# Gated linear attention with a max-out layer: state products of two batches on four array tiles, a turned head order, five permuting blocks, and a last output in two pieces

## The chip, the cores and the metric

The kernel runs on one core of a Trainium2 chip. A core has a matrix engine (TensorE, "PE" in the profile, with its weight loads as "PEld"), VectorE (DVE), ScalarE (ACT), GpSimd (POOL), SyncE (SP), which here only issues transfers, and 16 DMA engines. The metric is device microseconds (us) of one execution; lower is better. "The time before" is the median of three runs of the old kernel.

## What is computed

```python
def _attn_ref(q, k, v, f_logit):            # 4 batches, 8 heads, 768 positions, 48 per head
    f = 1.0 / (1.0 + np.exp(-f_logit))
    for t in range(S):
        state = f[:, :, t, :, None] * state + np.einsum('bhd,bhe->bhde', k[:, :, t], v[:, :, t])
        y[:, :, t] = np.einsum('bhd,bhde->bhe', q[:, :, t], state)

def _moe_ref(x, w1, w2, w_out):             # x: 3072 tokens by 384
    g = np.maximum(x @ w1, x @ w2)          # 384 by 1024
    return g @ w_out                        # 1024 by 384
```

The heads of a token stand side by side in x (8 times 48 is 384).

## The kernel before

**Windows.** The sequence is cut into 3 windows of 256 positions. A unit of work `s` is one window of one batch, `s = 4 * window + batch`, so there are twelve, and `s % 2` is the parity of the batch. Position pairs stand on 128 partitions (row p holds positions 2p and 2p+1), and a window has two halves `h` of 64 rows.

**Steps.** Every step is a letter. For each unit, `Lf Lk Lq Lv` (L111) load the four inputs, 128 rows by 8 heads by 96 numbers of float32, which is 1024 runs of 384 bytes. `E F G` (ACT, L207 to L217) make the gate's logarithm and `e` its pair sum; `C` (L222) sums it up with a triangular matrix; `X Z` (ACT) take exponentials of the sums; `i j K Q` (DVE or POOL) scale k and q into the padded bf16 tiles `kp` and `qp`, and `V` (L260) casts v into `vb`. Each head takes 64 columns there, of which 48 are used. `t u` (L264) transpose `kp` and `qp` in 16 matmuls each, and `U` copies both out of PSUM into `trs`. `A` (L280) multiplies keys with queries, `m` masks the product. `S` (L308) multiplies the carried state with the queries, `y` (L328) adds the masked product times v, `z` (L323) is a tiny DVE read of the last element that `S` wrote, which stands between `S` and `y`. `D n N` (L341 to L371) bring the state forward; `S` needs the state of the unit 4 earlier (its second half) and of its own first half. `Y` copies the finished y out of PSUM into `xT`.

**Layout of x.** Heads stand in four pairs. A pair takes 128 rows: head r of the pair sits at rows 64r to 64r+47, and 16 rows of each half are a gap. The first three pairs are the three 128-row blocks of the layer's contraction; the fourth pair's 2 times 48 rows are put into the gaps of these three, by step `M` (two DMAs inside SBUF, L401), or for the first two units by matmuls (`xf`, L391). The weights must stand in the same row order: `wp` (L495) permutes the rows of w1 minus w2 by matmuls, one for each (block of the result, block of the source) that meet, listed in `meets` (L186, 7 of them), for each of 4 quarters of the columns; `wx` (L463) does it for w2's transpose by copies.

**The layer.** max(a, b) is b plus relu(a - b), so `d` (L407, four steps a unit, 6 matmuls each) multiplies x with w1 minus w2, `r` (L415) takes the relu out of PSUM, and `o` (L425, two a unit) sums x times m2 (`wm`: w2 times w_out, L479) and the relu times w_out. `b` copies an output half of 128 by 384 out of PSUM, and `O` (L440) stores both halves of a unit.

**Array tiles.** `A`, `y` and `D` address the 128 by 128 array as four 64 by 64 tiles: rows by one index (r or h), columns by the other. In `S` the row tile and the column tile are the same index r, so of the four tiles only (0,0) and (1,1) are used:

```python
rows = slice(r * DP, r * DP + D)
nc.tensor.matmul(out=ys[s][h][r * DP:(r + 1) * DP, j, :], lhsT=st[rows, j, :],
                 rhs=t[rows, h, 1, j].rearrange("p a t -> p (a t)"), ...)
```

`S` of a unit is 16 matmuls of 128 columns, 8 for the first four units, which have no state in their first half: 160 in all.

**The order of the work.** `ORDER` (L20 to L54) is a list of 558 words: step, unit, engine (a, v, p, s) and, after the @, the PSUM bank or the input slot. Each engine works its own words off in this order, and one wait in an engine's queue holds up all that is behind it. SP issues all loads, nearly all `M` and all stores, in order. There are 25 input slots of one load each; the weights pass through them first.

Of the kernel before, what the change touches and what calls it, by code (L numbers as in the profile page):

```python
# [20 lines left out]
Lf0s@12 Lk0s@13 Lq0s@14 Lv0s@15 E0 Lf1s@16 F0 Lk1s@12 e0v G0 i0v C0@0 j0v Lq1s@17 X0 Z0 K0v Lv1s@18  # L21
Q0v t0@0 V0v u0@0 E1 Wb0s U0v@0 F1 Wa0s A0.0@0 e1p G1 Wb1s m0.0v@0 Wa1s i1p C1@2 Wo0s D0@4 Wo1s X1
j1v A0.1@0 Z1 K1p n0.0v V1a m0.1v@0 S0@6 Lf2s@16 z0v@6 Q1v y0 D1@0 t1@2 Yt0a@6 wc0p n1.0v wc1a u1@2
n1.1v U1v@2 wt0@0 N1.1p xf0@6 Y0a@6 ws0p n0.1v A1.0@2 A1.1@4 m1.0v@2 wx0a@0 wt1@1 ws1p wp0@6 m1.1v@4
wc2a S1@2 Lq2s@17 z1v@2 wq0v@6 y1 wt2@0 Yt1a@2 wp1@4 ws2v d0.0@6 wq1a@4 ws3p wx2v@0 xf1@2 d0.1@7
Y1a@2 wx1v@1 wp2@4 r0.0a@6 wc3v d1.0@2 Lk2s@0 wo0p wq2a@4 wt3@1 d1.1@3 wx3v@1 N0.1p wo1a d1.2@4 wo3p
Lf3s@1 r1.0v@2 wp3@0 wo2p d0.2@6 E2 wq3v@0 Lv2s@4 wm1@2 F2 Lk3s@5 d0.3@7 G2 e2v wn1a@2 j2v C2@3
wm0@0 X2 i2v Lf4s@6 Z2 K2v r0.1a@6 Lq3s@8 Q2v t2@2 d1.3@5 E3 wn0v@0 u2@2 F3 wm2@1 V2p Lf6s@10 U2v@2
G3 e3p r1.1a@4 D2@6 Lq4s@4 wn2v@1 A2.0@2 i3p C3@0 n2.0v o0.1@1 n2.1v X3 m2.0v@2 Lk4s@1 Z3 K3p E4
S2@6 A2.1@2 Lv3s@17 F4 o1.0@0 z2v@6 j3v G4 e4p m2.1v@2 E6 Lf5s@5 C4@4 Q3v t3@2 F6 y2 Lk6s@10 j4v  # L30
u3@2 Y2a@6 o0.0@5 e6p U3v@2 X4 M2s Z4 i4v A3.0@2 b1.0a@0 Lv4s@8 K4p b0.0v@5 C6@4 G6 Lq6s@6 o1.1@0
m3.0v@2 V3a X6 Lf8s@17 Q4v t4@2 Z6 A3.1@6 b0.1a@1 N2.1p b1.1v@0 D3@4 u4@2 E5 i6p n3.0v d2.0@0 Lk5s@4
n3.1v F5 U4v@2 d2.2@4 K6p d2.1@1 G5 Lq5s@5 m3.1v@6 d2.3@5 r2.0a@0 S3@2 V4p Lv6s@10 z3v@2 r2.1a@4 y3
j6v A4.0@0 D4@6 e5v Y3a@2 o2.0@4 n4.0v N4.0v E8 M3s Q6p n4.1v m4.0v@0 A4.1@6 F8 S4@2 Lv5s@8 C5@5
Lk8s@17 G8 m4.1v@6 o2.1@0 i5p Lf7s@6 b2.0a@4 Z5 z4v@2 e8v X5 y4 K5v C8@1 Y4a@2 d3.0@4 j5v t6@6
b2.1v@0 Q5p Z8 M4s t5@2 u6@6 d3.1@5 X8 U6v@6 V5a Lq8s@4 d3.2@0 Lk7s@1 N3.1p r3.0a@4 u5@2 Lq7s@8 D5@6
i8p U5v@2 d3.3@1 E7 N4.1p d4.0@4 Lf9s@5 n5.0v r3.1a@0 A5.0@2 N5.0v d4.1@5 n5.1v F7 m5.0v@2 N5.1p
d4.2@0 O1s V6p Lv8s@6 A5.1@6 r4.0a@4 d4.3@1 m5.1v@6 e7p Lv7s@0 S5@2 r4.1a@0 D6@4 K8p A6.0@6 z5v@2 y5
n6.0v O0s m6.0v@6 C7@0 Y5a@2 o4.0@1 Lq11s@10 N6.0p G7 n6.1v X7 j8v o3.0@2 b4.0a@1 Lf11s@17 Q8v Z7 E9
j7v M5s t8@0 A6.1@4 V8v F9 S6@6 i7p m6.1v@4 u8@0 Lq9s@6 o3.1@3 V7a e9p z6v@6 U8v@0 y6 K7v A8.0@0  # L40
D8@4 Y6a@6 o4.1@5 Q7p b3.0v@2 M6s m8.0v@0 b3.1a@3 C9@2 Lv11s@1 b4.1a@5 t7@6 n8.0v D7@0 Lk9s@8 Z9
u7@6 Lf10s@0 n7.0v d5.0@4 X9 N7.0p E11 d5.2@2 N6.1v N8.0p n7.1v Lv9s@5 d5.1@5 F11 j9v d6.0@0 j11v G9
d5.3@3 r5.0a@4 e11p U7v@6 Lk11s@17 d6.1@1 Q9p r5.1a@2 d6.2@4 r6.0v@0 O4s C11@6 Lv10s@4 d6.3@5 X11
A7.0@0 Z11 i9p O2s A7.1@2 o5.1@7 m7.0v@0 E10 K9p r6.1a@4 Lk10s@0 m7.1v@2 S7@0 F10 Lq10s@6 S8@4 z7v@0
A8.1@2 G11 e10p y7 o6.1@6 Y7a@0 i11v K11v M7s C10@0 Q11p m8.1v@2 o6.0@1 Z10 G10 z8v@4 X10 V11p y8
b6.0a@1 t11@2 b6.1v@6 Y8a@4 t9@0 u11@2 u9@0 o5.0@6 U11v@2 U9a@0 M8s j10v O6s d7.0@2 O3s Q10v b5.0a@6
A9.0@0 b5.1a@7 A9.1@4 i10p d7.1@3 m9.0v@0 V9a d7.2@6 K10p r7.0a@2 m9.1v@4 d8.0@0 d7.3@7 V10p d8.1@1
r7.1v@6 t10@4 r8.0a@0 D9@2 D11@3 u10@4 n9.0v A11.0@6 N7.1v U10a@4 A11.1@0 o7.0@2 n11.0v N11.0p N9.0v
d8.2@4 b7.0v@2 o7.1@3 m11.0v@6 m11.1v@0 d8.3@5 S9@6 r8.1a@4 b7.1v@3 S11@0 z9v@6 O7s D10@3 y9 z11v@0
# [9 lines left out]
def kernel(  # L59
# [22 lines left out]
    HD = H * D  # L82
    d_ff = moe_w1.shape[1]
# [3 lines left out]
    GAP = DP - D  # L87
# [23 lines left out]
    def load(nm, s, slot):  # L111
        w, b = divmod(s, B)
        src = sources[nm][b, :, w * W:(w + 1) * W, :].rearrange("h (p two) d -> p h (two d)", two=2)
        nc.sync.dma_start(out=slots[:, slot, :].rearrange("p (h x) -> p h x", h=H), in_=src)  # L114
        loaded[s][nm] = slots[:, slot, :].rearrange("p (h two d) -> p h two d", h=H, two=2)
# [52 lines left out]
    perm = consts.tile([C, KT, KT, C], BF16, name="perm")  # L168
    nc.gpsimd.memset(perm, 0.0)
    for j in range(KT):  # L170
        for r in range(2):
            first = D * (2 * j + r)
            for blk in range(KT):
                lo, hi = max(first, blk * C), min(first + D, (blk + 1) * C)
                if lo < hi:
                    nc.vector.tensor_copy(perm[:, blk, j, r * DP + lo - first:r * DP + hi - first],
                                          ident[:, lo - blk * C:hi - blk * C])
    for r in range(2):
        first = (2 * KT + r) * D - (KT - 1) * C
# [80 lines left out]
    def step_V(s, e):  # L260
        copy(e, pad("vb", s)[:, :, :, 0:D], by_parity(loaded[s]["v"]))
# [45 lines left out]

    def step_S(s, b):  # L308
        t = tr[s]
        ys[s] = [banks[:, b + h, :].rearrange("p (j t) -> p j t", j=NP) for h in range(2)]  # L310
        for h in range(2):
            if not has_state(s, h):
                continue
            st = state_before(s, h)
            for j in range(NP):
                for r in range(2):
                    rows = slice(r * DP, r * DP + D)
                    nc.tensor.matmul(  # L318
                        out=ys[s][h][r * DP:(r + 1) * DP, j, :], lhsT=st[rows, j, :],
                        rhs=t[rows, h, 1, j].rearrange("p a t -> p (a t)"),  # L320
                        start=(j == 0), stop=False, skip_group_check=True)
# [6 lines left out]
    def step_y(s):  # L328
        m, vb = at.pop(s), pad("vb", s)
        for j in range(NP):  # L330
            for par in range(2):
                for r in range(2):
                    for h in range(2):
                        rows = slice(h * HC, (h + 1) * HC)
                        first = j == 0 and par == 0 and not has_state(s, h)
                        nc.tensor.matmul(  # L336
                            out=ys[s][h][r * DP:(r + 1) * DP, j, :], lhsT=vb[rows, par, 2 * j + r, :],
                            rhs=m[rows, j // 2, r, j % 2, par, :], start=first,
                            stop=(j == NP - 1 and par == 1), skip_group_check=True)
# [85 lines left out]
    def step_o(g, par, b):  # L425
        cols = slice(par * C, (par + 1) * C)
        ps = banks[:, b, 0:HD]
        for kt in range(KT):
            nc.tensor.matmul(out=ps, lhsT=x_flat(g)[:, kt, cols], rhs=m2[:, kt, :],  # L429
                             start=(kt == 0), stop=False)  # L430
        for ff in range(FG):
            nc.tensor.matmul(out=ps, lhsT=gT[g][:, ff, cols], rhs=wo[:, ff, :],  # L432
                             start=False, stop=(ff == FG - 1))
# [29 lines left out]
    def store_w2T(q, e, b):  # L463
        h, x = divmod(q, 2)
        if h not in w2T:
            w2T[h] = work.tile([C, FG // 2, HD], BF16, name="ob", tag="ob", bufs=3)
        dst = w2T[h][:, 2 * x:2 * x + 2, :].rearrange("p f (k r i) -> p f k r i", k=KT, r=2)
        src, whole = w2_rows(b), 2 * KT * D
        copy(e, dst.rearrange("p f k r i -> p f (k r) i")[:, :, :, 0:D],
             src[:, :, 0:whole].rearrange("p f (g i) -> p f g i", i=D))  # L470
        for r in range(2):
            copy(e, dst[:, :, :, r, D:DP],
                 src[:, :, whole + r * D:whole + (r + 1) * D].rearrange("p f (i k) -> p f k i", k=KT))
# [21 lines left out]
    def permute(q, b):  # L495
        started = set()
        for i, (kt, blk) in enumerate(meets):
            bank, off = divmod(kt * QF, 512)
            nc.tensor.matmul(out=banks[:, b + bank, off:off + QF], lhsT=perm[:, blk, kt, :],  # L499
# [71 lines left out]
```

## Time and profile before

| what | value |
|---|---|
| time before, median of 3 runs | 146.18 us (145.88 to 146.31) |
| profiled execution | 145.86 us |
| its span, first to last instruction | 144.1 us |
| PE / DVE / ACT / POOL busy | 124.3 / 102.3 / 82.5 / 62.1 us |
| mean granted TensorE clock | 0.995 |
| DMA | 29.14 MB, 55607 packets, 50528 of them under 512 bytes |

The profile is of one execution. "Busy" is the union of an engine's instructions. A PE matmul's duration is that of the pipelined instruction, from its start to the end of its output, so that several overlap; what a matmul costs in a dense row is the distance from start to start, which the chain of waits gives. The profiled execution is 1.8 us longer than its span, and 0.32 us below the median of the runs.

### The profile page before, as it was taken

The page shows a single profiled execution, that of the slowest core. Times are in us where ns is not written, and L with a number is a line of the kernel's source. Part 1 is how long each engine was busy: PE and PEld are TensorE (multiplying, and loading weights), DVE is VectorE, ACT ScalarE, POOL GpSimd, SP SyncE. Part 2 cuts the span into 40 slices and gives each one's busy share as a digit, 9 for nine tenths or more (in the row PEclk, how much of TensorE's full clock was granted, in tenths as well). Part 3 has the DMA queues.
Part 4 walks back from the last instruction along what each step waited for, and adds up shares of the span by engine and source line. Part 5 has one row for each costly group of instructions (what it writes and reads, how often), then busy time and mean ns, then how long its engine had stood idle before and what let it go on. Part 6 is the DMA issues. An engine that isn't in the chain of part 4 may idle for free.

```text
span 144.1 us, 5338 instructions
## 1 busy us (share of the span) xinstructions
PE 124.3 (86%) x2332; PEld 91.0 (63%) x2332; DVE 102.3 (71%) x181; ACT 82.5 (57%) x120; POOL 62.1 (43%) x63
## 2 busy tenths in 40 slices
PE   0134888999999999996999999898999999999990
PEld 0024676886656676684866688566787777768650
DVE  5887888697888888955798965687985895316120
ACT  3636553887897968596585496666955211512300
POOL 7005758830783986294746159398501000000000
PEclk9999999999999999999999999999999999999998
DMA  4999999999999799699999569993420051005005
GB/s 117 268 262 267 386 384 376 310 245 268 261 266 258 179 275 241 176 251 265 265 290 272 137 165 265 273 337 83 148 89 5 21 209 25 0 14 223 0 6 212
DMA packets 55607, 29.14 MB, mean 202 GB/s; under 512 B 50528, under 2 KB 52512, under 8 KB 55584
## 3 DMA queue, kind: packets, MB, share of 16 engines
q1 hardware_dynamic: 55456, 28.76, 76.9%
q8 instruction: 18, 0.29, 0.9%
q10 hardware_dynamic: 128, 0.05, 0.1%
q14 instruction: 5, 0.04, 0.1%
HBM read 23.59 MB, written 4.72 MB: 197 GB/s over the span
## 4 chain that ended last, share of the span: by engine, by line
PE 52%; DMA 22%; ACT 9%; SPq 6%; issue 4%; DVE 2%; POOL 1%; ACTq 0%
PE banks L412 15%; PE banks L432 14%; DMA slots<-in_f_logit_dram 11%; DMA slots<-in_moe_w_dram 6%; PE banks L429 6%; DMA slots<-in_v_dram 5%; SPq L114 4%; PE banks L336 3%; PE banks L288 2%; PE banks L271 2%; PE banks L499 2%; PE banks L318 2%; PE banks L482 2%; ACT ell L213 2%; ACT one L217 1%
## 5 line engine op out<-in xcount | busy, mean ns | idle before, releaser
L412 PE MATMUL banks<-xT,wd 128*128 128x256 bf16 x288 | 35.3, 273 | 1.4 <-ACT gT L421 1.4
L432 PE MATMUL banks<-wo,gT 128*128 128x384 bf16 x192 | 35.1, 326 | 0.0
L296 DVE TENSOR_TENSOR at_m<-banks,mask 128x1024 bf16<-128x1024 f32 x24 | 28.8, 1219 | 5.4 <-PE banks L288 5.3
L412 PEld LDWEIGHTS <-wd 128*128 128x128 bf16 x288 | 27.0, 98 | 5.9 <-DMA xT<-xT 1.7
L421 ACT ACTIVATE gT<-banks 128x1024 bf16<-128x1024 f32 x19 | 19.1, 1020 | 16.5 <-PE banks L412 16.4
L432 PEld LDWEIGHTS <-gT 128*128 128x128 bf16 x192 | 18.8, 98 | 12.4
L103 DVE COPY ob<-banks 128x384 f32<-128x384 f32 (+2 forms) x20 | 8.3, 446 | 12.2 <-PE banks L432 10.8
L429 PE MATMUL banks<-m,xT 128*128 128x384 bf16 x72 | 15.7, 327 | 0.0
L103 ACT CAST xT<-banks 128x1024 bf16<-128x1024 f32 (+2 forms) x11 | 9.4, 857 | 10.9 <-PE banks L336 9.1
L103 ACT COPY ob<-banks 128x384 f32<-128x384 f32 (+2 forms) x16 | 7.1, 466 | 14.7 <-PE banks L432 11.3
L220 POOL TENSOR_TENSOR e<-ell 128x384 bf16<-128x384 f32 x8 | 8.8, 1094 | 15.1 <-ACT ell L213 14.4
L103 DVE COPY trs<-banks 128x2048 bf16<-128x2048 bf16 x10 | 12.2, 1222 | 3.7 <-PE banks L271 3.1
L209 ACT ACTIVATE gate<-slots 128x768 f32<-128x768 f32 x12 | 10.2, 849 | 7.6 <-DMA slots<-in_f_logit_dram 7.6
L254 POOL TENSOR_TENSOR kp<-slots,inv 128x768 bf16<-128x768 f32 x7 | 12.7, 1815 | 2.6 <-DVE slots L243 1.4
L371 POOL TENSOR_TENSOR st<-tmp_s,dec 128x192 bf16<-128x192 f32 x10 | 5.8, 587 | 14.4 <-DVE tmp_s L366 14.4
L288 PE MATMUL banks<-trs 48*64 48x128 bf16 x384 | 10.4, 227 | 1.5 <-DVE trs L103 1.3
L257 POOL TENSOR_TENSOR qp<-slots,dec 128x768 bf16<-128x768 f32 x5 | 9.6, 1913 | 4.1 <-DVE slots L247 4.1
L224 PE MATMUL banks<-e,u_inc 128*128 128x384 bf16 x12 | 4.3, 356 | 7.7 <-DVE e L220 6.7
L213 ACT ACTIVATE ell<-gate 128x768 f32<-128x768 f32 x12 | 10.1, 842 | 0.5
L336 PE MATMUL banks<-at_m,vb 64*64 64x128 bf16 x384 | 8.8, 225 | 1.6 <-DVE look L326 1.6
L288 PEld LDWEIGHTS <-trs 48*64 48x64 bf16 x384 | 7.1, 110 | 3.6 <-DVE trs L103 1.7
L336 PEld LDWEIGHTS <-vb 64*64 64x64 bf16 x384 | 7.1, 111 | 3.4 <-issue 3.3
(74 smaller groups left out, 189.5 us busy)
## 6 DMA issues: line engine op xcount, KB each, us to landing
slots<-in_f_logit_dram SPq DMA_DIRECT2D x12, 384.0 KB, 6.2
slots<-in_k_dram SPq DMA_DIRECT2D x12, 384.0 KB, 6.1
slots<-in_q_dram SPq DMA_DIRECT2D x12, 384.0 KB, 6.1
slots<-in_v_dram SPq DMA_DIRECT2D x12, 384.0 KB, 5.6
out_dram<-ob SPq DMA_DIRECT2D x12, 384.0 KB, 3.4
slots<-in_moe_w_dram SPq DMA_DIRECT2D x4, 768.0 KB, 9.1
slots<-in_moe_w_out_dram SPq DMA_DIRECT2D x2, 768.0 KB, 13.7
xT<-xT SPq DMA_DIRECT2D x18, 24.0 KB, 3.4
```

Source lines behind the costliest of these rows:

```text
L103: (nc.scalar.copy if e == "a" else engines[e].tensor_copy)(out, in_)
L209: nc.scalar.activation(flat(gate[s]), flat(loaded[s]["f"]), AF.Exp, bias=0.0, scale=-1.0)
L213: nc.scalar.activation(flat(ell[s]), flat(gate[s]), AF.Ln, bias=1.0, scale=1.0)
L254: engines[e].tensor_mul(pad("kp", s)[:, :, :, 0:D], by_parity(loaded[s]["k"]), both(inv[s]))
L257: engines[e].tensor_mul(pad("qp", s)[:, :, :, 0:D], by_parity(loaded[s]["q"]), both(dec[s][:, 0:HD].rearrange("p (h d) -> p h d", h=H)))
L288: nc.tensor.matmul(out=ps[h * HC:(h + 1) * HC, j % 2, par, :], lhsT=t[rows, h, 0, j, par, :], rhs=t[rows, h, 1, j].rearrange("p a t -> p ( ...
L296: nc.vector.tensor_mul(at[s][:, jj].rearrange("p r j a t -> p (r j) (a t)"), banks[:, b:b + 2, :].rearrange("p r (j x) -> p (r j) x", j=2) ...
L336: nc.tensor.matmul(out=ys[s][h][r * DP:(r + 1) * DP, j, :], lhsT=vb[rows, par, 2 * j + r, :], rhs=m[rows, j // 2, r, j % 2, par, :], start ...
L412: nc.tensor.matmul(out=ps[:, f, :], lhsT=wd[:, kt, ff * C:(ff + 1) * C], rhs=x_flat(g)[:, kt, :], start=(kt == 0), stop=(kt == KT - 1))
L421: nc.scalar.activation(dst, src, AF.Relu)
L429: nc.tensor.matmul(out=ps, lhsT=x_flat(g)[:, kt, cols], rhs=m2[:, kt, :], start=(kt == 0), stop=False)
L432: nc.tensor.matmul(out=ps, lhsT=gT[g][:, ff, cols], rhs=wo[:, ff, :], start=False, stop=(ff == FG - 1))
```

## The change

1. **Heads of odd batches are loaded turned by three.** The head that stands at place p of an odd unit is head p + 3 (mod 8). The load is two DMAs, of 5 and of 3 heads.
2. **State products of two units together, on four tiles.** Heads are paired anew: (0,1), (6,7), (4,3), (2,5). In an even unit the two heads of a pair stand at even and odd places, in an odd unit, by the turn, at odd and even ones. So the even unit uses array tiles (0,0) and (1,1), the odd one (1,0) and (0,1). The step `S` of the even unit now issues the matmuls of both units, alternating; `S` of the odd unit issues none and only takes its banks. The number of matmuls is the same.
3. **Five permuting blocks for seven.** With the new pairs only 5 (result, source) blocks meet. The fourth pair is dealt into the gaps in another way, and for it `V` gets a second copy of a quarter of its elements with the columns re-dealt (12 more copies in all), and `wx` has four copies for three.
4. **The last output half in two pieces.** `o11.1` makes 256 columns and `o11.2` 128, each with its own copy out of PSUM, and the last unit is stored in three DMAs (`P`) and not one.
5. **A new `ORDER`** of 562 words, with other engines for some steps, other slots and banks. The units go in pairs: 2 and 3, 4 and 5, and so on.

```diff
+    tiles = [(0, 1), (6, 7), (4, 3), (2, 5)]
+    TURN = 3
+    def spot(s, head):
+        pos = (head - TURN) % H if s % 2 else head
+        return pos // 2, pos % 2
...
-        nc.sync.dma_start(out=slots[:, slot, :].rearrange("p (h x) -> p h x", h=H), in_=src)
+        if s % 2:
+            nc.sync.dma_start(out=dst[:, 0:H - TURN, :], in_=src[:, TURN:H, :])
+            nc.sync.dma_start(out=dst[:, H - TURN:H, :], in_=src[:, 0:TURN, :])
+        else:
+            nc.sync.dma_start(out=dst, in_=src)
...
-    meets = [(0, 0), (0, 2), (1, 0), (1, 1), (1, 2), (2, 1), (2, 2)]
+    meets = [(0, 0), (0, 2), (1, 2), (1, 0), (2, 1)]
...
     def step_V(s, e):
+        dst, src = pad("vb", s), by_parity(loaded[s]["v"])
+        copy(e, dst[:, :, :, 0:D], src)
+        a, b = sorted(sum(p * x for p, x in zip(spot(s, head), (2, 1))) for head in tiles[KT])
+        copy(e, dst[:, :, a:b + 1:b - a, 0:D].rearrange("p two h (i k) -> p two h k i", k=KT),
+             src[:, :, a:b + 1:b - a, :].rearrange("p two h (k i) -> p two h k i", k=KT))
...
-            for j in range(NP):
-                for r in range(2):
-                    rows = slice(r * DP, r * DP + D)
+            for x in range(NP):
+                for g in (s, s + 1):
+                    for r in range(2):
+                        j, q_ = spot(g, tiles[x][r])
+                        rows = slice(q_ * DP, q_ * DP + D)
+                        nc.tensor.matmul(
+                            out=ys[g][h][r * DP:(r + 1) * DP, x, :], lhsT=state_before(g, h)[rows, j, :],
+                            rhs=tr[g][rows, h, 1, j].rearrange("p a t -> p (a t)"),
+                            start=(x == 0), stop=False, skip_group_check=True)
...
-            engines[e].dma_start(out=x[r * DP + D:(r + 1) * DP, 0:KT, :],
+            engines[e].dma_start(out=x[r * DP + D:(r + 1) * DP, 0:KT, :][:, ::1 - 2 * r, :],
...
+    def piece(g, i):
+        return (i, slice(0, HD)) if i == 0 or g < n_s - 1 else (1, (slice(0, 2 * C), slice(2 * C, HD))[i - 1])
...
+    def step_P(g, i, e):
+        par, m = piece(g, i)
+        w, b = divmod(g, B)
+        row = b * S + w * W
+        engines[e].dma_start(out=out[row:row + W, :].rearrange("(p two) m -> p two m", two=2)[:, par, m],
+                             in_=obs[g][:, par, m])
```

The new order in the places that the prediction speaks of (words of other steps left out):

```
Lf2 Lf3 Lk2 Lq2 Lq3 E2 F2 Lk3 E3 e2p Lv2 C2 d1.2 K2v Lv3 d1.3 wm1 Lf4 C3 t2 Lf5 u2 wm2 i3p U2v Lk4 K3p A2.0 A2.1 V2a
o1.0 Lv4 Q3p V3a D2 Lq4 D3 t3 u3 o0.0 Lk5 U3v Lf7 A3.0 C4 S3 S2 Lq5 A3.1 y2 o0.1 Lv5 C5 y3 t4 D4 Lq7 u4 o1.1 A4.0 Lf6
A4.1 d2.0 Lk7 d2.2 Lk6 d2.1 d2.3 O0 d3.0 Lv7 C7 d3.1 Lq6 t5 D5 u5 o2.0 Lf9 d3.2 A5.1 O1 A5.0 Lv6 d3.3 o2.1 Lf8 S5 S4
t7 C6 y5 y4 u7 o3.0 A7.0 E9 D7 t6 o3.1 F9 u6 d4.0 E8 d5.0 F8 d4.1 d5.2 r4.0v d5.1 d5.3 r5.0a ...
... o10.1 r11.1a o10.0 o11.0 b10.0v b10.1v O10s o11.1 b11.0a P11.0s o11.2 b11.1v P11.1s b11.2a P11.2s
```

In the old order the loads after the weights go `Lf2 Lq2 Lk2 Lf3 Lv2 Lk3 Lf4 Lq3 Lf6 Lq4 Lk4 Lv3`, and the list ends `o11.0 r10.1a o10.1 b11.0v o10.0 o11.1 b10.0v b10.1v O10s b11.1a O11s`.

More of the change, by code (lines that the diff above doesn't have):

```diff
@@ L26 @@
[L26 to L37, printed above, removed]
@@ L498, in permute @@
             bank, off = divmod(kt * QF, 512)
-            nc.tensor.matmul(out=banks[:, b + bank, off:off + QF], lhsT=perm[:, blk, kt, :],
+            nc.tensor.matmul(out=banks[:, b + bank, off:off + QF], lhsT=perm[:, i, :],
                              rhs=wdn[q][:, blk, :], start=bank not in started,
```

137 lines of the change are left out of this document (74 added, 63 removed).

## The prediction

> **What bounds the kernel now.** First the head of the page: busy shares, and the span in 40 slices of 3.6 us.
>
> ```profile
> span 144.1 us, 5338 instructions
> ...
> PE 124.3 (86%) x2332; PEld 91.0 (63%) x2332; DVE 102.3 (71%) x181; ACT 82.5 (57%) x120; POOL 62.1 (43%) x63
> ...
> PE   0134888999999999996999999898999999999990
> ...
> PEclk9999999999999999999999999999999999999998
> DMA  4999999999999799699999569993420051005005
> ```
>
> PE is full from slice 7 (25 us) to the last but one, at full clock. The DMA engines are full from slice 1 to about slice 25 (94 us). So two resources press: transfers decide when the inputs of a unit are there, and PE has work for nearly the whole time behind that. Next the arrivals, in the timeline (start, duration, what; in brackets the idle time and what ended it).
>
> ```profile
> 30.00 0.84 ACT L209 ACTIVATE gate<-slots 128x768 f32<-128x768 f32 x1 [0.41 <-DMA slots<-in_f_logit_dram]
> ...
> 35.67 1.20 POOL L103 CAST vb<-slots 128x768 bf16<-128x768 f32 x1 [5.50 <-DMA slots<-in_v_dram]
> ...
> 65.30 0.84 ACT L209 ACTIVATE gate<-slots 128x768 f32<-128x768 f32 x1 [0.71 <-DMA slots<-in_f_logit_dram]
> ...
> 67.09 0.81 PE L412 MATMUL banks<-xT,wd 128*128 128x256 bf16 x6 [1.43 <-ACT gT L421]
> ```
>
> Unit 2's f comes at 30.0 us, its v as the fourth load after that at 35.67: 5.67 / 4 = 1.42 us a load. The last two rows show how an arrival reaches PE: ACT stood before a gate, the relu behind it in ACT's queue was late, and PE stood 1.43 us. Last the chain of waits, whose pieces (start, length, what) give each step's cost in dense work:
>
> ```profile
> 26.05 0.33 PE banks L394 x6
> ...
> 30.18 0.76 PE banks L499 x7
> 30.94 0.66 PE banks L412 x6
> 31.59 1.30 PE banks L482 x8
> ...
> 33.55 0.16 PE banks L224
> 33.71 0.09 PE banks L227 x4
> ...
> 38.28 0.37 PE banks L350 x32
> ...
> 76.92 0.45 PE banks L318 x16
> 77.36 0.34 PE banks L271 x16
> ...
> 79.60 0.60 PE banks L336 x32
> ...
> 103.23 0.57 PE banks L288 x32
> ...
> 114.04 1.00 PE banks L318 x29
> ...
> 138.47 0.49 PE banks L429 x3
> 138.96 1.31 PE banks L432 x8
> ```
>
> So `d` costs 0.66, `wm` 1.30, `C` 0.25, `D` 0.37, `S` 0.45 (16 matmuls), `t` or `u` 0.34, `y` 0.60, the two `A` of a unit 0.57, `o` 1.80. All PE steps of the old order at these costs: 48 `d` 31.7, 24 `o` 43.2, twelve units' `C`, `t`, `u`, `A`, `y` 25.2, `D` 3.7 (the last four units have one half), `S` 4.5, `wp` 3.0, `wm` 3.9, and 36 matmuls of `wt` and `xf` at 0.055, 2.0: about 117 us. The last matmul ends at 138.96 + 1.31 = 140.3. The 23 us between are mostly the start. Of the work 17 us stand ahead of unit 2's `C` in the order, so from there (33.55) on 100 us of work take 106.7: some 6 us are lost. Work taken off PE is therefore nearly all gained, unless the inputs are late.
>
> **The change, part by part.**
>
> *State products.* Now 0.45 / 16 = 28.1 ns a matmul (34.5 in the row at 114.04). The nearest row for four tiles is `A`, also 48 rows and 128 columns: 0.57 / 32 = 17.8 ns. 160 matmuls times 10.3 ns: **-1.7 us**. Bounds: 0, if four go no faster than two (a loss is out, as neither number nor size grows), and 160 * (28.1 - 11.6) = -2.6, at `D`'s 0.37 / 32. I take `A`, which has the same shape.
>
> One thing differs from `A`: there the two row tiles write two banks, in `S` the row tiles 0 and 1 write one bank, on different partitions, before as after. The 128-column matmul on the whole array takes 0.33 / 6 = 55 ns (L394), and `S` 28.1, so the two already run side by side in one bank. The Trainium skill, TensorEngine Tiling (Array Packing), Gotcha 1, says that different row tiles cannot access the same PSUM bank at the same time; by that `S` would cost 55 ns a matmul now, and the trace does not agree. If such a limit came in with four tiles, this term would be 0 and the time the 145.8 us of the third rival.
>
> *Permuting blocks.* 0.76 / 7 = 0.109 us each, 2 fewer in 4 quarters: **-0.9 us**, bounds 0 and -0.9. It is gained ahead of `C2`, which in its turn waits for f: 30.0 + 0.84 + 0.84, and 1.0 for `e2` on POOL (L213 and L220 below), make 32.7 us at the least; with latencies I take 32.9, against 33.55. So PE is there 0.7 us sooner, and what it saves beyond that is `d` and `wm` work done early.
>
> *Inputs of units 2 and 3 together.* In the new order v of unit 2 is the sixth load after f (before: the fourth), v of unit 3 the seventh: 30.0 + 7 * 1.42 = 39.9 us, and `V3a`, on ACT, then takes its copy and the second one. The costs are in the groups of instructions (line, engine, output and input, count; busy us, mean ns of one; idle before).
>
> ```profile
> L254 POOL TENSOR_TENSOR kp<-slots,inv 128x768 bf16<-128x768 f32 x7 | 12.7, 1815 | 2.6 <-DVE slots L243 1.4 <-ACT inv L234 1.0
> L103 DVE COPY trs<-banks 128x2048 bf16<-128x2048 bf16 x10 | 12.2, 1222 | 3.7 <-PE banks L271 3.1 <-ACT gT L421 0.6
> ...
> L213 ACT ACTIVATE ell<-gate 128x768 f32<-128x768 f32 x12 | 10.1, 842 | 0.5
> L257 POOL TENSOR_TENSOR qp<-slots,dec 128x768 bf16<-128x768 f32 x5 | 9.6, 1913 | 4.1 <-DVE slots L247 4.1
> ...
> L220 POOL TENSOR_TENSOR e<-ell 128x384 bf16<-128x384 f32 x8 | 8.8, 1094 | 15.1 <-ACT ell L213 14.4 <-POOL st L371 0.6
> L243 POOL TENSOR_TENSOR slots<-slots,one 128x384 f32<-128x384 f32 x8 | 8.0, 998 | 2.5 <-ACT one L217 1.1 <-DMA slots<-in_k_dram 0.9 <-ACT ob L103 0.4
> ...
> L103 ACT COPY ob<-banks 128x384 f32<-128x384 f32 x13 | 6.2, 483 | 14.7 <-PE banks L432 11.3 <-DVE st L371 3.3
> ...
> L371 POOL TENSOR_TENSOR st<-tmp_s,dec 128x192 bf16<-128x192 f32 x10 | 5.8, 587 | 14.4 <-DVE tmp_s L366 14.4
> ...
> L103 ACT CAST vb<-slots 128x768 bf16<-128x768 f32 x5 | 4.2, 837 | 0.1
> ...
> L103 ACT CAST xT<-banks 128x256 bf16<-128x256 f32 x2 | 0.7, 372 | 2.8 <-PE banks L336 2.8
> ```
>
> The copy of 192 elements is between nothing and the 0.37 of 256 elements on ACT; I take 0.3. `D3` cannot start before 39.9 + 0.84 + 0.3 = 41.0. PE, dense from `C2` at 32.9, has two `d`, two `wm`, `C3`, `t2`, `u2`, `A2`, `o1.0` and `D2` ahead of it, 7.6 us: it is there at 40.5. `u3` waits for `i3`, `K3` and `Q3`, all on POOL behind k of unit 3: 30.0 + 5 * 1.42 = 37.1, and 1.0 + 1.8 + 1.9 make 41.8, and PE is there at about 41.7. With the latencies between I put the stop at **+1.1 us**; bounds 0 and 2.8, the two loads by which v2 is later, with no cover by `o1.0`.
>
> *V's second copies.* 12 copies, 8 on ACT at 0.3 and 4 on POOL at up to 0.59: 2.4 us each. ACT is busy 57% and POOL 43%; the waits of both hide them, except where `D` stands behind `V` as above. Uncovered they are at most 0.3 each on PE. The fourth copy of `wx` is on DVE in the time of the weights, in which the f of unit 2 is awaited: 0.
>
> *Split loads.* 24 loads become two DMAs; the bytes and the 384-byte runs stay.
>
> ```profile
> L114 SPq DMA_DIRECT2D slots<-in_q_dram x12: 368/1323/3923, 1.9 to 93.2; - x12
> ...
> 1.25 0.56 SPq L114 DMA_DIRECT2D slots<-in_k_dram  x1
> ...
> 31.29 1.31 SPq L114 DMA_DIRECT2D slots<-in_k_dram  x1
> ```
>
> The first row has the durations in ns (least, median, most). An issue costs 0.37 to 0.56 us where nothing is in its way (the least; the kernel's second load) and 1.3 in the dense stretch, where the queue takes a load only as fast as it moves one. Two free issues, 0.74 to 1.12, are still below 1.42. Cost **0**; if the cover is gone, 0.37 to 0.56 a load on everything behind it on SP, loads, `M` and stores alike (second rival).
>
> *The last output.* Both orders keep 1.8 us of matmuls for the last half: 11 of 256 columns at 0.109 and 11 of 128 at 0.055. Behind the last matmul stand the copy, the store, and what ends the program.
>
> ```profile
> out_dram<-ob SPq DMA_DIRECT2D x4, 384.0 KB, 2.5
> ...
> xT<-xT ACTq DMA_DIRECT2D x2, 24.0 KB, 1.9
> ```
> ```profile
> 142.00:142.50 0.50, 0.00 (x0) 0.00 (x0) 0.00 (x0) 0.00 (x0) 0.00 (x0) 1.00 1.03 412
> 142.50:143.00 0.50, 0.00 (x0) 0.00 (x0) 0.00 (x0) 0.00 (x0) 0.00 (x0) 0.73 0.24 92
> ```
>
> In the windows (last three columns: clock, DMA share, GB/s) data flow at full rate up to 142.5 and are through by 142.6, 1.5 us before the end; a smaller last piece shortens the part ahead of that. Copy: 0.483 for 384 columns, 0.372 for 256, so 0.26 for 128 (the same slope): -0.2. Store: 2.5 us from issue to landing for 384 KB; 1.9 for the smallest transfer of the trace. The new last piece has 64 KB, nearest the small one: 2.0, -0.5; but 128 KB leave just ahead of it, +0.1. Sum **-0.6**, bounds -0.8 and 0.
>
> *Other changes of place.* The rest of the order is new too. I find no cost in it: the pair's `S` has `o0.0`, `o2.0`, 3.9 us of `d`, `d6` and `o7.1` between the later unit's `u` and its use, more than the 1.22 us of a copy of `trs` on DVE, and a `t`, `C`, `d` or `o` between `S` and most `y`. Value 0, open by about 1.5 us either way, as the 6 us that PE now loses after 33.55 can shrink or grow.
>
> **Sum.** -1.7 - 0.9 + 1.1 + 0 - 0.6 = -2.1 us on the profiled execution of 145.86 (span 144.1, 1.8 around it): 143.8, span 142.0. That execution is 0.32 below the median of the runs, 146.18; I give the median: **144.1 us**.
>
> **The rivals.**
>
> 1. *Late inputs swallow it.* `o1.0` needs all of m2 and unit 1's relus; if these are late, nothing covers v2, the stop is 2.8 us, and what `wp` saved is waited away too (+0.4): 146.2. For: 5.50 us of POOL waiting for one v. Against: PE has `d` and `wm` there in both orders.
> 2. *The split loads hold up the stream*, slower. By `E8` 13 odd loads have gone since f2; if each costs SP its second issue of 0.56 openly, f8 comes 7.3 us late. Unhindered it is number 27 behind f2 (stores counted): 30.0 + 27 * 1.42 = 68.3. ACT's turn for `E8` comes, by the order, with 37.4 us of PE work done behind `C2` (11 `d` 7.3, 8 `o` 14.4, 2 `wm` 2.6, 5 `C` 1.2, 12 `t` and `u` 4.1, 9 halves of `A` 2.6, 5 `D` 1.9, `S` of a pair and a half 0.9, 4 `y` 2.4): 32.9 + 37.4 + 1.1 = 71.4. Slack 3.1 us; beyond it the relus behind `E8` are late as in the rows at 65.30 and 67.09, microsecond for microsecond: +4.2, 148.3. It turns slower from a stream 5.2 us late (3.1 and the gain of 2.1). Against: two free issues are shorter than a load's 1.42.
> 3. *Four tiles bring nothing*: a pair's `S` stays at 28 ns a matmul. 144.1 + 1.7 = 145.8. Against: `A`.
>
> **How the numbers follow.** About 0.3% (0.44 us) is what a measurement of this kernel can tell from no change. Forecast 0.66, all of it faster; rival 1 0.10 and rival 3 0.08, within 0.3%; rival 2 0.16, slower. The range goes down to 142.3 (the far bounds of `S` and the stop, half the open place term) and up to 147.0, which takes in rivals 1 and 3 and the lower half of rival 2; the upper half and a few hundredths below are left out.
>
> **What would show it.** Right: `S` of a pair at about 0.57 to 0.6 us in the chain for 32 matmuls; 20 permuting matmuls; `C2` near 32.9; the last matmul near 138.8 and 3.2 us from it to the end of the span, against 3.8; the issues on L114 at about half of 1.3 each in the dense stretch. Wrong: a stop of over 2 us before `D2` or `D3`; ACT waiting for f at unit 8 or 9 with relus and PE behind it; 28 ns a matmul in `S`; or PE losing clearly more than 6 us after `C2` at places that I did not name.

## The result, and the profile after

The changed kernel takes **143.55 us** in the median (142.10 to 145.11), the old one in runs on the same chip 145.87 (144.87 to 147.47). The ratio is 0.9834, with a 95% interval of 0.9806 to 0.9861: **2.4 us faster**, where 2.1 were forecast, of 144.1. The runs of one kernel differ by more than a microsecond, so each ratio below stands with its interval, and a difference to the changed kernel is the difference of two ratios times 145.9, with the half widths of the intervals joined as the root of the sum of their squares. The medians are of all runs, while each ratio leaves out the slow runs of a kernel (over 1.5% above its fastest), so that the ratio of e0 rests on two of its six runs and that of e11 on seven of twelve. The profiled execution of the changed kernel took 144.36 us, 0.8 above its median; a second one, of the unaltered kernel (e0), took 141.79. What both show is the kernel; where they differ, it is the run.

First the page: busy shares and the 40 slices, now of 3.57 us.

```profile
span 142.6 us, 5440 instructions
...
PE 122.4 (86%) x2335; PEld 89.7 (63%) x2335; DVE 96.6 (68%) x188; ACT 88.8 (62%) x131; POOL 63.2 (44%) x69
...
PE   0145369998999899989996999999999999999992
...
DMA  4999999999999976998869989379910350105023
```

PE has 1.9 us less to do, ACT 6.3 more. Slices 5 and 6 of PE are 3 and 6, where 8 and 8 stood, and that is 14 to 21 us, the start, read below. The DMA engines stay busy to slice 29 (103 us), where slice 27 (97 us) was the last full one before, with dips on the way (15, 16, 21, 26), as before (14, 17, 23, 24). The chain of waits (start, length, what) has the steps that the prediction named:

```profile
25.30 0.67 PE banks L530 x5
...
31.11 0.73 ACT wo L109
31.84 0.75 ACT gate L219
32.62 0.85 ACT ell L223
...
33.54 1.01 POOL e L230
...
34.59 0.32 PE banks L234
...
84.72 0.45 PE banks L335 x32
...
118.90 0.57 PE banks L335 x32
...
139.35 0.46 PE banks L454 x8
139.83 0.27 ACT ob L109
```

Read it from the bottom. The last matmul ends at 139.8 and the span at 142.6: 2.8 us of tail for 3.8. A pair's `S` (L335) is 0.45 to 0.57 us for 32 matmuls, 14 to 18 ns each, where 28 to 35 stood. A permuting step is 5 matmuls. But `C2` (L234) stands at 34.59 and not at 32.9: the gate of unit 2 runs at 31.8 behind the last weight cast on ACT, and no longer waits for its f.

Three stretches give the balance of the two profiled executions (timeline and chain): start to `C2`, 33.4 before and 34.6 after, +1.2; `C2` to the last matmul, 106.9 and 105.2, -1.7; tail, 3.8 and 2.8, -1.0. In e0 they are 34.05, 103.2 and 2.7. The start is late in both profiles of the new kernel; the middle is where runs differ.

### The profile page after: what moved, and what is told of

Same layout as the page of the kernel before. It is cut to its first block, busy times and chain, and to the rows that moved or that the text cites. A ratio compares the mean times of both kernels' runs of the same rounds, so it can differ in the third digit from the quotient of the medians.

```text
span 142.6 us, 5440 instructions
## 1 busy us (share of the span) xinstructions
PE 122.4 (86%) x2335; PEld 89.7 (63%) x2335; DVE 96.6 (68%) x188; ACT 88.8 (62%) x131; POOL 63.2 (44%) x69
## 4 chain that ended last, share of the span: by engine, by line
PE 58%; DMA 13%; ACT 10%; DVE 6%; SPq 4%; POOL 3%; issue 3%; DVEq 0%; ACTq 0%; POOLq 0%
PE banks L454 16%; PE banks L430 16%; DMA slots<-in_v_dram 9%; PE banks L451 7%; PE banks L302 4%; PE banks L354 4%; DMA xT<-xT 4%; ACT vb L109 3%; PE banks L285 3%; DVE qp L267 2%; SPq L125 2%; PE banks L368 2%; POOL e L230 1%; PE banks L335 1%; PE banks L530 1%
## 5 line engine op out<-in xcount | busy, mean ns | idle before, releaser
L454 PE MATMUL banks<-wo,gT 128*128 128x384 bf16 (+2 forms) x200 | 35.3, 320 | 0.0
L109 DVE COPY ob<-banks 128x384 f32<-128x384 f32 (+4 forms) x28 | 9.2, 375 | 13.7 <-PE banks L454 9.5
L264 POOL TENSOR_TENSOR kp<-slots,inv 128x768 bf16<-128x768 f32 x9 | 16.4, 1826 | 1.8 <-ACT inv L244 0.8
L253 POOL TENSOR_TENSOR slots<-slots,one 128x384 f32<-128x384 f32 x9 | 9.4, 1050 | 14.8 <-ACT one L227 9.6
L451 PE MATMUL banks<-m,xT 128*128 128x384 bf16 (+2 forms) x75 | 15.9, 321 | 0.0
L109 POOL CAST vb<-slots 128x768 bf16<-128x768 f32 (+1 forms) x8 | 8.5, 1058 | 12.9 <-DMA slots<-in_v_dram 12.7
L109 ACT COPY ob<-banks 128x384 f32<-128x384 f32 (+1 forms) x13 | 5.9, 468 | 12.9 <-PE banks L454 12.9
L109 ACT CAST vb<-slots 128x768 bf16<-128x768 f32 (+1 forms) x16 | 10.6, 674 | 2.5 <-DMA slots<-in_v_dram 2.2
L441 DVE TENSOR_SCALAR gT<-banks 128x1024 bf16<-128x1024 f32 x5 | 6.0, 1221 | 6.6 <-PE banks L430 6.6
L267 DVE TENSOR_TENSOR qp<-slots,dec 128x768 bf16<-128x768 f32 x9 | 10.3, 1148 | 0.3
```

The costliest lines, as they stand in the source:

```text
L109: (nc.scalar.copy if e == "a" else engines[e].tensor_copy)(out, in_)
L253: engines[e].tensor_mul(even, even, one[s])
L264: engines[e].tensor_mul(pad("kp", s)[:, :, :, 0:D], by_parity(loaded[s]["k"]), both(inv[s]))
L267: engines[e].tensor_mul(pad("qp", s)[:, :, :, 0:D], by_parity(loaded[s]["q"]), both(dec[s][:, 0:HD].rearrange("p (h d) -> p h d", h=H)))
```

## The experiments

Each kernel is the changed one with the edit shown, unless it says otherwise; they ran against the old kernel in turn. The changed kernel itself ran beside e1 to e3 only, as e0; e4 to e7 and e8 to e11 ran on two other chips, where the old kernel is the common measure.

### e0: the unaltered kernel again

> The changed kernel again, unaltered, as the level for the three runs beside it. Both theories: 143.5 us, ratio to the old kernel 0.983 or so.

144.01 us, ratio 0.9772 (0.9674 to 0.9870). The timeline of PE, waits in brackets, first of the profiled changed kernel, then of e0:

```profile
34.59 0.32 PE L234 MATMUL banks<-e,u_inc 128*128 128x384 bf16 x1 [0.38 <-POOL e L230]
47.81 0.42 PE L302 MATMUL banks<-trs 48*64 48x128 bf16 x16 [0.63 <-DVE at_m L310]
...
76.20 4.76 PE L430 MATMUL banks<-xT,wd 128*128 128x256 bf16 x42 [1.57 <-DMA xT<-xT]
```
```profile
34.05 0.32 PE L234 MATMUL banks<-e,u_inc 128*128 128x384 bf16 x1 [0.37 <-POOL e L230]
47.20 0.42 PE L302 MATMUL banks<-trs 48*64 48x128 bf16 x16 [0.64 <-DVE at_m L310]
54.51 3.70 PE L430 MATMUL banks<-xT,wd 128*128 128x256 bf16 x30 [0.22 <-DMA xT<-xT]
```

The waits at 34 and 47 are the same to 0.01 us: they belong to the order. The 1.57 us at 76.2 do not: `d4` waits for the two times 24 KB that `M4` moves inside SBUF, and in e0 they are there in time. In the chain that move takes 5.01 us from issue to landing in the one, 3.74 in the other.

### e1: the state products unit by unit

```diff
-            for x in range(NP):
-                for g in (s, s + 1):
+            for g in (s, s + 1):
+                for x in range(NP):
```

> The changed kernel with the two loops of the state products exchanged: all matmuls of the even unit, then all of the odd one, so that two array tiles work at a time and not four. Same matmuls, same place in the order. Theory of the prediction (PE work is the bound, four tiles save 28.1 - 17.8 ns on 160 matmuls): a pair takes 0.9 to 1.0 us in the chain and the time rises by 1.7 us (up to 2.2, since the changed kernel's pairs took 0.45 to 0.57). Rival (the gain comes from the new order, and the state products stand where PE has time): the matmuls get slower by as much, but the time rises by less than 0.6 us.

144.32 us, ratio 0.9875 (0.9802 to 0.9949): 0.6 +- 1.1 above the changed kernel, which tells nothing by itself. The profile says that the edit did not undo what it meant to: a pair is 0.48 to 0.60 us in the chain, and the groups of instructions (busy us, mean ns) give 4.3 us for `S`.

```profile
L335 PE MATMUL banks<-trs,st 48*64 48x128 bf16 x160 | 4.3, 228 | 0.1
```

Eight matmuls on one pair of tiles, followed by eight on the other, run beside each other nearly as well as alternating ones. To take the four tiles away, the turn has to go (e4).

### e4 and e5: no turn, with cut and with whole loads

```diff
-    TURN = 3
+    TURN = 0
...
-            nc.sync.dma_start(out=dst[:, 0:H - TURN, :], in_=src[:, TURN:H, :])
-            nc.sync.dma_start(out=dst[:, H - TURN:H, :], in_=src[:, 0:TURN, :])
+            nc.sync.dma_start(out=dst[:, 0:5, :], in_=src[:, 0:5, :])
+            nc.sync.dma_start(out=dst[:, 5:H, :], in_=src[:, 5:H, :])
```

That is e4. In e5 the odd units are loaded as the even ones, by one DMA.

> The changed kernel with a turn of 0, the odd batches' loads still cut into 5 and 3 heads: all heads stand at the places of the old kernel, so that both units of a pair use the array tiles (0,0) and (1,1) only. Number and place of all instructions are those of the changed kernel. (The exchange of loops did not do this: 8 matmuls on one pair of tiles still overlapped with the next 8 on the other pair, and PE's busy time on the line rose from 3.6 to 4.3 us only, where the old kernel had 6.8.) Theory (PE is the bound, four tiles save what the chain shows): busy time on the line about 6.8 again, a pair 0.9 to 1.0 us in the chain, the time 1.7 to 2.0 us above the changed kernel, about 145.4. Rival (the new order gives the gain): less than 0.6 us above.

> As the run before, with a turn of 0, and each odd load in one DMA again: 24 issues fewer on SP than there. Theory (a second issue is shorter than the time a load takes to move, so it is hidden): within 0.4 us of the run with the cut loads. Rival (SP is late in the stretch from 50 to 75 us, where in the changed kernel the odd loads' issues stood back to back and the DMA engines fell to 170 to 200 GB/s): 1 us or more faster than the run with the cut loads, and the f of unit 8 earlier by several us.

e4: 145.67 us, ratio 0.9962 (0.9923 to 1.0001), **1.9 +- 0.7 us above the changed kernel**. The order and the number and size of loads, copies and matmuls are the same; the heads of the odd units stand at other places, and with them `S` is on other tiles. The groups of instructions of before, of the changed kernel and of e4:

```profile
L318 PE MATMUL banks<-trs,st 48*64 48x128 bf16 x160 | 6.8, 223 | 0.7 <-ACT gT L421 0.6
```
```profile
L335 PE MATMUL banks<-trs,st 48*64 48x128 bf16 x160 | 3.6, 227 | 0.0
```
```profile
L335 PE MATMUL banks<-trs,st 48*64 48x128 bf16 x160 | 6.4, 227 | 0.9 <-DVE at_m L310 0.6 <-DVE tmp_s L384 0.2
```

The mean of one matmul stays at 223 to 227 ns; what shrinks is the distance from one start to the next, and with it the line's busy time, 6.4 to 3.6 between e4 and the changed kernel. In the chain a pair of units takes 0.89 to 1.01 us in e4 and 0.45 to 0.57 in the changed kernel: 0.44 for 32 matmuls, 2.2 for all 160.

e5: 144.65 us, ratio 0.9873 (0.9818 to 0.9927). It stands 1.3 +- 1.0 us *below* e4, by nothing but 24 DMAs fewer. In e4 DVE waited 2.9 us for a late q (0.4 in e5), and `S` of units 6 and 7 stood twice; in e5 it ran through (timelines; e4 first):

```profile
84.53 0.90 PE L335 MATMUL banks<-trs,st 48*64 48x128 bf16 x18 [0.65 <-DVE at_m L310]
85.66 0.58 PE L335 MATMUL banks<-trs,st 48*64 48x128 bf16 x14 [0.22 <-DVE tmp_s L384]
```
```profile
83.33 1.06 PE L335 MATMUL banks<-trs,st 48*64 48x128 bf16 x32
```

Against the changed kernel e5 is only 0.6 +- 0.9 us slower. So the turn as a whole, the tiles that it gains and the cut loads that it costs, is not clear of nothing.

### e11: the old kernel with cut loads

To see the cut without the new order, the old kernel's odd loads were cut 5 + 3.

```diff
-        nc.sync.dma_start(out=slots[:, slot, :].rearrange("p (h x) -> p h x", h=H), in_=src)
+        dst = slots[:, slot, :].rearrange("p (h x) -> p h x", h=H)
+        if s % 2:
+            nc.sync.dma_start(out=dst[:, 0:5, :], in_=src[:, 0:5, :])
+            nc.sync.dma_start(out=dst[:, 5:H, :], in_=src[:, 5:H, :])
+        else:
+            nc.sync.dma_start(out=dst, in_=src)
```

> The kernel before with the loads of its odd units cut into five and three heads, without the turn: 24 more issues on SP, nothing else. The prediction put the cut at nothing: 145.6 to 146.1, ratio within 0.2% of 1. The experiments so far (unsplit against split loads without the turn: 1.3 us, give or take 0.9) say that it costs about 1.3 us where the loads stand close on SP: ratio 1.005 to 1.013, 146.6 to 147.8, with SP's issues of the pieces at 0.35 to 0.56 us and later landings of f, k and q between 60 and 85 us.

Ratio 1.006 (1.0008 to 1.0112): **0.9 +- 0.8 us slower than the old kernel**. The prediction's nothing is outside the interval. The waits of POOL, old kernel and e11 (us in total, times, longest):

```profile
POOL slots L243 <- DMA slots<-in_k_dram: 0.9, 1, 0.9
```
```profile
POOL slots L248 <- DMA slots<-in_k_dram: 4.3, 3, 2.0
```

And the timelines of ACT and PE in e11 (the relu that PE waits for stands right behind the gate on ACT):

```profile
91.91 0.84 ACT L214 ACTIVATE gate<-slots 128x768 f32<-128x768 f32 x1 [2.03 <-DMA slots<-in_f_logit_dram]
```
```profile
93.71 0.49 PE L323 MATMUL banks<-trs,st 48*64 48x128 bf16 x11 [1.04 <-ACT gT L426]
```

In the old kernel the same gate waited 1.63 us, at 91.29, and the same `S` 0.64. So the second rival's way is there (late f, late gate, late relu behind it in the queue, late PE), but with 0.4 us here. The larger new wait of PE in e11 is 1.1 us at 106.95, for a masked product that PE did not wait for before; it comes behind POOL's late k's, though the way from there to PE is not shown. Both together are 1.5 of the 1.9 us by which the two profiles' spans differ. The size, about 0.9, is a quarter of the 4.2 us that the rival was given.

### e2: seven permuting blocks

```diff
-        for i, (kt, blk) in enumerate(meets):
+        for i, (kt, blk) in enumerate(meets + [(0, 1), (2, 2)]):
```

(`perm` gets two blocks of zeros, which add nothing to the result.)

> The changed kernel with two permuting blocks of zeros added to each of the four quarters, so 28 matmuls again and not 20; the result does not change. Theory of the prediction (PE dense up to unit 2's C): 8 * 0.109 = 0.9 us slower. Rival (in that stretch the copies of the weights, on ACT and DVE, or the arrival of f set the pace): under 0.4 us slower.

145.39 us, ratio 0.9959 (0.9922 to 0.9996): 1.8 +- 0.7 us above the changed kernel. The chain has the blocks at their old cost:

```profile
24.70 0.87 PE banks L530 x7
...
29.79 0.78 PE banks L530 x7
```

Eight matmuls more at 0.109 are 0.87 us, just below the interval's lower end of 1.1. The trace shows these 0.87 by themselves, from the first block to `C2`:

```profile
24.63 0.94 PE L530 MATMUL banks<-wdn,perm 128*128 128x256 bf16 x7
...
34.87 0.32 PE L234 MATMUL banks<-e,u_inc 128*128 128x384 bf16 x1 [0.38 <-POOL e L230]
```

That is 10.24 us. In the changed kernel it is 9.36 (25.23 to 34.59), and in e0 9.36 too (24.69 to 34.05), so the eight matmuls cost 0.88 there. When the first block comes varies from profile to profile. Of the other 0.9, one move of `xT` is waited for by 1.02 us at 59.15, where the changed kernel waits 0.15; whether it is such waits, which shift from run to run, or something else of the edit, stays open.

### e3: the last output in one piece

```diff
-        return (i, slice(0, HD)) if i == 0 or g < n_s - 1 else (1, (slice(0, 2 * C), slice(2 * C, HD))[i - 1])
+        return (i, slice(0, HD))
...
-b11.0a@6 P11.0s o11.2@6 b11.1v@7 P11.1s b11.2a@6 P11.2s
+b11.0a@6 b11.1a@7 O11s
```

> The changed kernel with the last output half in one piece of 384 columns and the last unit stored in one DMA. Theory of the prediction: +0.6 us, the copy 0.2 longer and the store 0.4. By the profile of the changed kernel, where 2.8 us lie between the last matmul and the end of the span and not 3.8: +1.0 us. Rival (only the end of PE's work moved the time): 0 to 0.2.

144.50 us, ratio 0.9902 (0.9861 to 0.9942): 1.0 +- 0.7 us above the changed kernel. In its chain the last matmul ends at 138.67, and the span of 142.4 ends 3.7 us later, as before the change.

```profile
137.34 1.31 PE banks L454 x8
138.67 0.48 ACT ob L109
```

### e8: no second copy of V

```diff
-        a, b = sorted(sum(p * x for p, x in zip(spot(s, head), (2, 1))) for head in tiles[KT])
-        copy(e, dst[:, :, a:b + 1:b - a, 0:D].rearrange("p two h (i k) -> p two h k i", k=KT),
-             src[:, :, a:b + 1:b - a, :].rearrange("p two h (k i) -> p two h k i", k=KT))
```

> Leaves out the second V copy of every unit (the 12 strided copies that put the fourth product's rows in the other order: 8 on ACT, 518 ns each, 4 on POOL, 967 ns each), so the fourth pair of heads of each unit is computed from rows in the wrong order; nothing else changes. Theory of the prediction (the copies lie beside other work): within 0.4 us of the changed kernel, 143.2 to 143.9, and ACT's and POOL's busy time lower by 4.1 and 3.9 us. Rival (they stand in ACT's queue ahead of gates and copies that PE waits for, as V0 and V2/V3 do): up to 8 x 0.52 = 4.1 us less work of ACT, of which the three places at the start and at 40.6 to 43.2 count, 1 to 1.5 us: 142.0 to 142.6, with the first permuting block before 24.7.

142.84 us, ratio 0.9750 (0.9687 to 0.9814): 1.2 +- 1.0 us below the changed kernel. What left, in the changed kernel's groups with forms apart:

```profile
L109 ACT CAST vb<-slots 128x192 bf16<-128x192 f32 x8 | 4.1, 518 | 0.3
L109 POOL CAST vb<-slots 128x192 bf16<-128x192 f32 x4 | 3.9, 967 | 0.2
```

The copies cost 0.52 and 0.97 us each, where 0.3 and at most 0.59 were put. The time fell between the two theories; zero is outside the interval, if barely, and by the quotients of the medians it is 0.7 us. The rival's place at the start fails: the first permuting block came at 24.99 us, between the 25.23 and the 24.69 of the changed kernel's two profiles. One place is certain: the products `D2` and `D3`, which in the changed kernel wait a little for V3's second copy (PE's timelines, changed kernel first):

```profile
42.59 1.01 PE L368 MATMUL banks<-vb,kp 64*64 64x48 bf16 x64
43.53 0.41 PE L285 MATMUL banks<-ident,kp 64*128 64x64 bf16 x16
```
```profile
42.34 0.72 PE L365 MATMUL banks<-vb,kp 64*64 64x48 bf16 x64
43.00 0.41 PE L282 MATMUL banks<-ident,kp 64*128 64x64 bf16 x16
```

To the next step it is 0.94 us with the copy and 0.66 without: 0.28. Where the rest comes from is not settled.

### e9 and e10: U1 on DVE, and v6 loaded later

```diff
-U1a@4
+U1v@4
```

e10 has besides `Lv6s@16` behind `M5s`, where the changed kernel has it in front of `M4s`.

> The copy of unit 1's transposed forms back on DVE, as in the kernel before (1.22 us there, 1.87 us on ACT in the changed kernel). If the start's chain of V0, D0, U1 and A1 on ACT is what delays the second batch of C's from the forecast 32.9 to 34.6, the first permuting matmul comes 0.6 us sooner (24.6 for 25.2), C2 at 34.0, and the time is about 143.0. Rival: C2 waits for the gate behind the casts on ACT (E2's gate ran at 31.7), whatever the start does: C2 stays within 0.2 of 34.6 and the time within 0.3 of 143.55; DVE has its own queue there and gives 0.6 us back, so a slower result is possible by the same size.

> The kernel of e9 with the load of v6 behind the moves M4 and M5 on SP's queue, where the changed kernel has it in front. If the wait of PE for unit 4's moved rows (1.57 us in the profile of the changed kernel, 0.2 to 1.1 in its repeats) comes from the loads in front of the move in the DMA queues, the move lands in about 2 to 3 us for 5.0, the wait goes, f8 comes up to 1.4 us sooner, and the time is 0.3 to 1.0 below e9's. Rival: the move is queued behind all that was issued in the 7 us before, v7 and f8 among it, so one load less changes the landing by less than 1.4 of 5.0 us and PE has other late inputs right behind it (k9, q9): the time within 0.3 of e9's, or above it, if v6 then comes late to its copy.

Ratios 0.9886 (0.9830 to 0.9942) and 0.9887 (0.9834 to 0.9941): each 0.8 +- 0.9 us above the changed kernel, and no different from each other. The timeline of e9 shows why U1 on DVE brings nothing:

```profile
19.47 0.64 PE L302 MATMUL banks<-trs 48*64 48x128 bf16 x16 [0.67 <-DVE trs L109]
19.90 0.32 PE L335 MATMUL banks<-trs,st 48*64 48x128 bf16 x2
20.87 0.64 PE L335 MATMUL banks<-trs,st 48*64 48x128 bf16 x14 [0.65 <-DVE st L386]
```

PE waits 0.67 us for the copy, where it waited 0.97; the 1.2 us that it takes of DVE are then missing for `st`, and `S` waits for that. So nothing speaks for DVE here, and the theory that U1 on ACT delays `C2` falls: `C2` stands at 34.98 in e9.

In e10 the wait at 76 is gone, and so it is in e9, with no load moved; and in both a wait as long stands 17 us earlier (1.62 us at 59.60 in e9, put down there to a step of DVE), here in e10:

```profile
59.75 0.81 PE L430 MATMUL banks<-xT,wd 128*128 128x256 bf16 x6 [1.53 <-DMA xT<-xT]
```

That is `M3`'s move. Which of the moves comes late changes from profile to profile, so that taking one load out of the way of one of them settled nothing.

### e6 and e7: moves on ACT's queue

```diff
-M4s
+M4a
...
-M5s
+M5a
```

That is e7; e6 has `M2` and `M3` on ACT too.

> The changed kernel with the gap transfers M of units 2 to 5 issued by ACT and not by SP. In SP's queue they wait for a finished y, and the loads behind them wait too; in the profiles of the changed kernel PE waited 0.2 to 1.6 us for such a transfer before a d. Theory (SP's order holds up loads and M, and that is the part of the time that swings from run to run): 0.5 to 1.5 us faster, no PE wait on xT<-xT, f of units 8 and 9 earlier. Rival (eight issues of 0.6 us on ACT delay its copies and relus by as much): no change or up to 1 us slower.

> As the run before, but only M of units 4 and 5 on ACT. Theory: the PE wait ahead of unit 4's d goes (0.2 to 1.6 us), the loads of units 6 to 9 are as late as in the changed kernel: 0 to 1 us faster than it. Rival: no change, since the relus behind the f of unit 8 take the place of the wait.

e6: 145.72 us, ratio 0.9950 (0.9910 to 0.9989), 1.7 +- 0.7 above the changed kernel. e7: 143.55 us, ratio 0.9800 (0.9740 to 0.9860), not distinguishable from it (-0.5 +- 1.0). In e7's table of DMAs (count, KB, median us from issue to landing) the moves on ACT's queue come no sooner:

```profile
xT<-xT SPq DMA_DIRECT2D x14, 24.0 KB, 2.5
xT<-xT ACTq DMA_DIRECT2D x6, 24.0 KB, 4.3
```

The medians are not of the same moves, but PE's waits for moves in e7 say no better, where the changed kernel waits once, 1.6 us:

```profile
PE banks L430 <- DMA xT<-xT: 2.5, 3, 1.1
```

So here a queue of its own didn't help the moves. The Trainium skill, DMA: Bandwidth & Descriptors, Queues, rings and completion order, says that each DMA engine takes turns between the queues that have work, packet by packet; by that one would expect a move on ACT's queue to pass the loads that wait on SP's. These rows don't show that, though only six moves went that way (ten in e6: 3.2 us, and 2.3 on SP). And ACT pays for the issues. The timeline of ACT in e6:

```profile
72.31 2.25 ACTq L422 DMA_DIRECT2D xT<-xT  x2
74.67 0.84 ACT L219 ACTIVATE gate<-slots 128x768 f32<-128x768 f32 x1 [1.48 <-issue]
```

## Why the prediction was right, and where it was not

**State products: right.** Forecast -1.7, measured -1.9 +- 0.7 by e4 (-2.2 by the chain). The chain has 0.45 us for 32 matmuls at best, 14 ns, where `A`'s 17.8 was taken; 14 ns is a quarter of the 55 ns of a whole-array matmul of 128 columns. The Trainium skill's rule that was weighed (TensorEngine Tiling (Array Packing), Gotcha 1: row tiles don't reach one PSUM bank at once) would have left 28 ns or more; the trace does not agree, with four tiles as little as with two. The third rival is out.

**Permuting blocks: the work went, the step after it failed.** 0.109 us a matmul holds: e2's trace has 0.88 for the eight matmuls, as forecast, and its time 1.8 +- 0.7. What failed is the step that puts `C2` at 32.9, where it would wait for f. Unit 2's gate does not wait for f, but stands behind the last weight cast on ACT (31.11 and 31.84 in the chain). PE itself got there at 34.2, with one `d` less behind it than in the old order (six for seven, 0.66 us) and 0.87 less of permuting, and still 1.2 us later: the start lost 2.7 us more than before. The waits of PE up to 33 us name the place, the old kernel first:

```profile
PE banks L271 <- DVE kp L254: 1.6, 1, 1.6
PE banks L288 <- DVE trs L103: 1.3, 1, 1.3
...
PE banks L271 <- DVE qp L257: 0.3, 1, 0.3
```
```profile
PE banks L285 <- DVE kp L264: 3.2, 2, 1.6
PE banks L302 <- DVE trs L109: 1.5, 1, 1.5
PE banks L302 <- ACT trs L109: 1.0, 1, 1.0
PE banks L285 <- DVE qp L267: 0.9, 1, 0.9
```

For kp, qp and trs PE stood 3.2 us, now 6.6. Some other waits went; all together, without the first one for `e`, which is alike, they were 5.8 and are 7.3, and `C2`'s own 0.38 comes to it. That is 1.9 of the 2.7; the rest is in gaps too small for the view. In the old order unit 1's transposes stand behind unit 0's `S`, `y` and `D` (at 17.63 us), and its kp and qp are there by then; now units 0 and 1 go side by side, the transposes come at 15.60, ahead of that work, and PE waits for each unit's kp, qp and trs in its turn. The prediction took the start as it was and looked at the order only from `C2` on; its value of 0 for the other changes of place left this out.

**The stop at `D2` and `D3`: 0.3 and not 1.1.** PE takes `D2` and `D3` from 42.59 on, 2.1 us later than the 40.5 that was worked out, and loses 0.28 there (e8). In the chain V3's second copy, a row of 0.53 us at 42.65, ends where the last products of `D3` begin. The step that failed is the one behind the stop, a v that comes late: ACT took V2 at 40.60 right behind the copy of `wm2`'s result, for which it had waited on PE, and waited for no v. Nor was it PE's late start that hid a late v, at least not within 1.5 us: in the profiles `D2` begins anywhere from 42.04 (e0) to 43.52 (e5), and from there to the next step it is 0.94 or 0.95 in each of them but e8. No profile has a PE that comes sooner. The first rival, a stop of 2.8 there, is out.

**Split loads: 0 was wrong.** e11 says 0.9 +- 0.8, e4 against e5 1.3 +- 1.0; together about 1 us. The issues themselves were as forecast, 0.37 to 0.54 us where nothing is in the way. But to set two free issues against the 1.42 of a load compares means, while an input is late at single places: the q in e4, f and k in e11. In the changed kernel f8 was issued at 68.58 and its gate waited for it until 75.81, where 68.3 had been worked out for the landing; without the cuts (e5) it was issued at 67.79, so by these two profiles the cuts account for 0.8 us of that. What makes the rest stays open: between 32 and 68.6 us SP waited 0.9 us at moves and over 6 at loads, for other engines' steps. The second rival was right that late loads reach PE, at about a quarter of its price. The way that it named is seen in e11; in the changed kernel's profile PE waits for no relu.

**V's second copies: 0 was probably wrong by about as much** (1.2 +- 1.0, of which 0.28 at `D2` and `D3` is seen in the trace); the estimate of one copy was too low by 0.2 us on ACT and 0.4 on POOL.

**Last output: -0.6 forecast, -1.0 measured** (e3, and the tails of 3.8 and 2.8). The copy is 0.27 for the 0.26 put; from the copy's end to the span's end it is 2.5 us for 3.3. So the store was mis-sized: -0.8 for the -0.4 put (-0.5, and +0.1 for the 128 KB that leave ahead).

**The sum.** Measured one by one: tiles -1.9, permuting -1.8, tail -1.0, cuts about +1, second copies +1.2: -2.5, where the whole is -2.4. With the 0.88 that the trace shows for permuting it would be -1.6. Five measurements of +- 0.7 to 1.0 do not close a balance, and no run takes the new order, with its later start, apart from the rest. What they do show is the picture: three gains of 3.8 to 4.7 us, about half of which two side costs of the turn and of the new pairing, both put at nothing, seem to give back. That the forecast came out so near is in part luck: the stop, put at 1.1 and found to be 0.3, stood in for them.

**Faster still?** None of the variants is measurably faster than the changed kernel and computes the same; e8, the only one clearly below it, leaves work out and gives a wrong result.

## What to carry to other kernels

Count a change's side works (extra copies, extra DMA issues) at their own measured cost even on engines that are half idle: here two such terms, put at zero with a good-sounding cover, took back about half of the gain by the middle values of the runs. Compare an issue's price with the slack at the places where an engine waits for its input, not with the mean pace of a stream. And when an order is new, walk the waits of the start again: here it lost 2.7 us that the forecast did not have.

## What the runs showed of the hardware that was not expected

- Matmuls of 48 rows, 64 columns of weights and 128 columns of data start every 14 ns on four array tiles (0.45 us for 32), and every 15 where eight on one pair of tiles are followed by eight on the other (e1, 0.48).
- A copy of 128 by 192 elements with a re-dealt inner order took 0.52 us on ACT, more than the 0.37 that a plain copy of 256 took, and 0.97 us on POOL.
- A 24 KB move inside SBUF took 1.9 us from issue to landing at the least and 5.0 at the place where it was issued right behind two loads; on another engine's queue the median was 4.3 in e7 (six moves) and 3.2 in e6 (ten).
